# One-token attention decode: the last head's wo in sixteen short transfers on ScalarE's queue during block 30

## The chip, the cores and the metric

One core of a Trainium2 chip runs the kernel. The metric is the device time of one execution in microseconds (us). Five engines take part: TensorE (PE, whose weight loads are shown apart as PEld), VectorE (DVE), ScalarE (ACT), GpSimd (POOL) and SyncE (SP). Bulk data move on the core's 16 DMA engines; SP and ACT issue transfers to them, each on a queue of its own (q1 and q10 in the profile).

## The reference

One token's attention over a cache of 65,536 positions with 16 query heads and 8 KV heads, mixed by a gate with a small token MLP:

```python
q = (x @ wq) ...                       # x: 1 x 448, wq: 448 x 4096
scores = einsum("bhqd,bhkd->bhqk", q, k) * Dh ** -0.5   # Dh = 256, 2 query heads for each KV head
o = einsum("bhqk,bhkd->bhqd", softmax(scores), v)
a = o.reshape(1, 1, 16 * 256) @ wo     # wo: 4096 x 448
b = token_mlp(B_x)                     # layernorm, w1, gelu, w2
g = sigmoid((x * gate_w).sum(-1))
return g * a + (1 - g) * b
```

All inputs are bf16. K and V together are 537 MB; everything else is small beside them.

## The kernel before

The cache is cut into 32 blocks of 16,384 positions (four for each KV head). For each block, SP loads K into two thirds of `k_all` and V into `vt`; DVE transposes K in eight steps (`transposes`, L410), PE forms the scores (`scores`, L418), `softmax` (DVE, PE, and the exp on ACT at L506) updates a running maximum and sum, and PE multiplies by V (`pv`, L438).

Blocks 0 to 29 run in a loop, two for each turn; blocks 30 (`L - 1`) and 31 (`L`) are written out behind it. The order of each engine's instructions is the program's order (`seq` ties each to the one before). SP's transfers of the tail are, in that order: V rows 0 to 48 of block 30 (L135), the two halves of K of block 31 (L127, one into each free third of `k_all`), V rows 48 to 128 of block 30 (L135), seven V pieces of block 31 (`load_v_last`, L161: 64, 32, 16, 8, 4, 2 and 2 rows of each partition), wo of the last head (`load_wo`, L152), and the result (L705).

wo of the other heads comes in a wide form (`load_wo_wide`, L144) and is spread by PE and two casts on ACT (`spread_wo`, L563 and L567). Head 14's is spread directly behind the loop, by `spread_wo(0)`. The last head's is loaded in place, into the second half of `wo_sb`:

```python
            load_v_last(L)
            load_wo(HQ - 1, 1)
```

It is read by the last matmuls (L697): PE finishes the products of the last V pieces (`columns`, L463), DVE scales them into `oT` (L691), PE multiplies `oT` by `wo_sb`, DVE and ACT copy the two halves of the row (L703, L704), and SP writes it out.

A built program gives each transfer of SP and ACT one of eight completion counters in turn, in the order of the program, and makes a transfer wait until the earlier one on its counter has landed.

Of the kernel before, what the change touches and what calls it, by code (L numbers as in the profile page):

```python
# [14 lines left out]
HQ = 16  # L15
# [18 lines left out]
def kernel(  # L34
# [15 lines left out]
    nc = tc.nc  # L50
# [12 lines left out]
    def seq(ins):  # L63
        e = ins.ins.engine
        if e in last:
            tc.add_manual_dep(
                ins.ins,
                last[e],
                mybir.DependencyInfo(
                    mybir.DependencyClass.NoSync, mybir.DependencyReason.DATA  # L70
                ),
                reason="program order",
            )
        last[e] = ins.ins.name
        return ins
# [7 lines left out]
    wo_sb = kvpool.tile([128, REP, 2, D], BF16, name="wo_sb")  # L83
# [42 lines left out]
    def load_k(n, h, slot):  # L126
        seq(nc.sync.dma_start(  # L127
            out=slots[slot], in_=rows("k", n)[:, h * KP:(h + 1) * KP, :]
        ))
# [4 lines left out]
    def load_v(n, j0=0, j1=VP):  # L134
        seq(nc.sync.dma_start(out=vt[:, j0:j1, :], in_=rows("v", n)[:, j0:j1, :]))  # L135
# [15 lines left out]
    def load_wo(h, r):  # L151
        seq(nc.sync.dma_start(  # L152
            out=wo_sb[:, r],
            in_=A_wo.rearrange("(h p c) n -> h p c n", p=128, c=2)[bass.ds(h, 1)].rearrange(
                "o p c n -> (o p) c n"
            ),
        ))

    def load_v_last(n):
        for j0, j1 in LAST:  # L160
            seq(nc.sync.dma_start(  # L161
                out=v_half[j0 // KP][:, j0 % KP:(j1 - 1) % KP + 1, :],
                in_=rows("v", n)[:, j0:j1, :],
            ))
# [3 lines left out]
        out=wq_t[:, :], in_=A_wq[DM:D, :].rearrange("r (h n) -> (r h) n", h=2)  # L168
# [8 lines left out]
    for n0, n1 in ((0, D // 2), (D // 2, D)):  # L177
        seq(nc.scalar.dma_start(
            out=gw[:, n0:n1], in_=gate_w.rearrange("(o n) -> o n", o=1)[:, n0:n1]
# [14 lines left out]
        out=val[:], in_=rowsel[:, :, :, 0:NI], op=ALU.add, axis=AXIS.XY  # L194
    ))
    fst = const.tile([128, 2, REP], FP32)
    for e in range(2):
        seq(nc.vector.tensor_reduce(
            out=fst[:, e, :], in_=rowsel[:, :, :, e:e + 1], op=ALU.add, axis=AXIS.XY
# [3 lines left out]
        out=par[:], in_=ident_f[:].rearrange("p (a r) -> p r a", r=REP), op=ALU.add, axis=AXIS.X  # L203
# [3 lines left out]
        out=nval[:], in0=val[:], scalar1=-scale, scalar2=None, op0=ALU.mult  # L207
# [7 lines left out]
        out=same[:], in_=val[:].unsqueeze(1).to_broadcast([128, 64, REP])  # L215
# [8 lines left out]
        out=sel[:],  # L224
        in_=ident.rearrange("p (w k) -> p w k", w=NW).unsqueeze(2).to_broadcast([128, NW, NQ, 32]),
# [7 lines left out]
        out=xrr[:], in_=xr[:, DM:D].unsqueeze(2).to_broadcast([1, D - DM, 2])  # L233
    ))
    x_col = hd_ps[:, 40:44]
    for k in range(3):
# [13 lines left out]
        out=xtm[:], in0=par[:], scalar1=x_col[:, 3:4], scalar2=None, op0=ALU.mult  # L250
# [19 lines left out]
        out=veps[:], in0=mv[:, 1:2], scalar1=1e-5, scalar2=None, op0=ALU.add  # L270
# [5 lines left out]
    for _ in range(2):  # L276
# [3 lines left out]
            out=ntmp[:], in0=ntmp[:], scalar1=-0.5, scalar2=1.5, op0=ALU.mult, op1=ALU.add  # L280
# [3 lines left out]
        out=h_bc, in0=xf, scalar1=mv[:, 0:1], scalar2=rstd[:, 0:1],  # L284
        op0=ALU.subtract, op1=ALU.mult,
    ))
    for b in range(NF):
        seq(nc.scalar.activation(
            out=gel[b], in_=h_bc, func=ACT.Gelu_apprx_tanh,
# [33 lines left out]
    for k in range(2):  # L323
        seq(nc.vector.tensor_copy(
            out=qq[:, :, :, k, :], in_=qq_ps.rearrange("p (w g r) -> p w g r", g=HKV, r=REP)
# [30 lines left out]
    def mixer_tail():  # L356
        seq(nc.vector.tensor_scalar(
            out=gate[:], in0=ez[:], scalar1=1.0, scalar2=None, op0=ALU.add
        ))
        seq(nc.vector.reciprocal(out=gate[:], in_=gate[:]))  # L360
        seq(nc.vector.tensor_copy(out=b2f[:], in_=b2b[:]))
        seq(nc.vector.tensor_scalar(
            out=y_sb[:], in0=y_ps, scalar1=b2f[0:1, 0:1], scalar2=None, op0=ALU.add
        ))
        seq(nc.vector.tensor_scalar(
            out=rest[:], in0=y_sb[:], scalar1=gate[0:1, 0:1], scalar2=None, op0=ALU.mult
        ))
        seq(nc.vector.tensor_tensor(out=rest[:], in0=y_sb[:], in1=rest[:], op=ALU.subtract))
# [57 lines left out]
    def score_block(e, pair, hooks={}, order=FORWARD):  # L426
        for k, i in enumerate(order):
            transposes(pair, i)
            scores(e, i, k == 0, k == NI - 1)
            if k in hooks:  # L430
                hooks[k]()

    def pv(n, ip, jjs=range(NJ), tile=None, dst=pv_ps, last_ip=NI // 2 - 1):
        pT = pT_tiles[n % 2]
        v = vt[:, 32 * ip:32 * (ip + 1), :] if tile is None else tile
        for jj in jjs:
            grp = jj % 4
            seq(nc.tensor.matmul(  # L438
                dst[32 * grp:32 * grp + 2 * REP, :, :],
                lhsT=pT[:, 32 * jj + 2 * REP * ip:32 * jj + 2 * REP * (ip + 1)],  # L440
                rhs=pairs(v)[:, :, jj, :],
                start=(ip == 0 and jj < 4),
                stop=(ip == last_ip and jj >= NJ - 4),
                tile_position=(0, 32 * grp),
            ))

    def pv_one(n, i):
        ip, e = divmod(i, 2)
        for jj in range(NJ):
            grp = jj % 4  # L450
            seq(nc.tensor.matmul(
                pv_ps[32 * grp:32 * grp + 2 * REP, e, :],
                lhsT=pT_tiles[n % 2][:, 32 * jj + 2 * REP * ip:32 * jj + 2 * REP * (ip + 1)],
                rhs=vt[:, NJ * i + jj, :],
                start=False, stop=False,
                tile_position=(0, 32 * grp),
            ))
# [60 lines left out]
    def accumulate(e, src=pv_ps):  # L518
        seq(nc.vector.scalar_tensor_tensor(  # L519
            out=acc[:], in0=acc[:], scalar=al_tiles[e][:, 0:1], in1=src[:, :, :],  # L520
            op0=ALU.mult, op1=ALU.add,
        ))
# [37 lines left out]
    def spread_wo(r):  # L560
        for c in range(2):
            for u in range(WS):
                seq(nc.tensor.matmul(  # L563
                    wo_ps[c], lhsT=steps[:, WS - u:WS - u + 128], rhs=wo_in[:, 2 * u + c, :],
                    start=(u == 0), stop=(u == WS - 1),
                ))
            seq(nc.scalar.copy(out=wo_sb[:, r, c, :], in_=wo_ps[c]))  # L567
# [13 lines left out]
    def gate_column():  # L581
        seq(nc.tensor.matmul(
            sm_ps[:, 200:201], lhsT=ones_f[0:1, :], rhs=gate[0:1, 0:1], start=True, stop=True
        ))
        seq(nc.vector.tensor_copy(out=gcol[:], in_=sm_ps[:, 200:201]))
# [47 lines left out]
                products(e)  # L633
    last.clear()
    spread_wo(0)
    mixer_tail()
    gate_column()
    result_base()

    for n in (L - 1, L):  # L640
        if n < L:
            score_block(0, (0, 1), order=UPPER_FIRST)
        else:
            score_block(1, (2, 1), {2: lambda: pv(L - 1, 0), 3: lambda: pv_one(L - 1, 2)})
        if n == L - 1:
            load_v(n, 0, 48)
            load_k(L, 0, 2)
            load_k(L, 1, 1)
            load_v(n, 48, VP)
        else:  # L650
            load_v_last(L)
            load_wo(HQ - 1, 1)
        if n < L:
            softmax(n % 2)
        else:
            def rest_base():
                for k in range(2):
                    seq(nc.tensor.matmul(
                        f_rows[k], lhsT=ident_f[0:1, 0:1], rhs=base[0:1, k * MC:(k + 1) * MC],
                        start=True, stop=False, tile_position=(0, 32 * k),  # L660
                    ))
                pv(L - 1, 2, range(4, NJ))

            softmax(n % 2, [lambda: pv_one(L - 1, 3), lambda: pv(L - 1, 2, range(4)), rest_base])
            seq(nc.vector.tensor_scalar(
                out=lsv[:], in0=val[:], scalar1=lsum[:, 0:1], scalar2=None, op0=ALU.mult
            ))
            pv(L - 1, 3)
            accumulate((L - 1) % 2)
            seq(nc.tensor.matmul(  # L670
                sm_ps[:, 456:456 + REP], lhsT=ones_f[:, :], rhs=lsv[:, :], start=True, stop=True
            ))
            seq(nc.vector.reciprocal(out=rdv[:], in_=sm_ps[:, 456:456 + REP]))
            seq(nc.vector.tensor_scalar(
                out=rdv[:], in0=rdv[:], scalar1=gcol[:, 0:1], scalar2=None, op0=ALU.mult
            ))
# [5 lines left out]
    for c in range(2):  # L682
# [9 lines left out]
        out=oT[:], in0=o_last, in1=rdv[:].unsqueeze(1).to_broadcast([128, 2, REP]), op=ALU.mult  # L692
# [43 lines left out]
```

## Time and profile before

| | |
|---|---|
| median of 3 runs | 1263.91 us (1263.62 to 1263.98) |
| span of the profiled execution, first to last instruction | 1261.8 us |
| beside the span, to the median | 2.1 us |
| PE, DVE, ACT busy | 824.5, 711.8, 75.7 us |
| DMA | 544.36 MB, mean 431 GB/s |

The profile's page stands on one execution; only its span is given, so its own time is taken as the span and the 2.1 us that the median has beside it. Shares of the chain are shares of the span in which the work that ended last was waiting for the thing named. "DMA share" in the windows is the mean busy share of the 16 DMA engines; it can go a little over 1 in a short stretch, since a packet counts where it starts. A DMA row with three figures gives the count, the size, and the us from issue to landing.

### The profile page before, as it was taken

The page shows a single profiled execution, that of the slowest core. Times are in us where ns is not written, and L with a number is a line of the kernel's source. Part 1 is how long each engine was busy: PE and PEld are TensorE (multiplying, and loading weights), DVE is VectorE, ACT ScalarE, POOL GpSimd, SP SyncE. Part 2 cuts the span into 40 slices and gives each one's busy share as a digit, 9 for nine tenths or more (in the row PEclk, how much of TensorE's full clock was granted, in tenths as well). Part 3 has the DMA queues.
Part 4 walks back from the last instruction along what each step waited for, and adds up shares of the span by engine and source line. Part 5 has one row for each costly group of instructions (what it writes and reads, how often), then busy time and mean ns, then how long its engine had stood idle before and what let it go on. Part 6 is the DMA issues. An engine that isn't in the chain of part 4 may idle for free.

```text
span 1261.8 us, 12358 instructions
## 1 busy us (share of the span) xinstructions
PE 824.5 (65%) x4818; PEld 331.2 (26%) x4818; DVE 711.8 (56%) x755; ACT 75.7 (6%) x163; POOL 4.8 (0%) x9
## 2 busy tenths in 40 slices
PE   4757467575666756577566766658656576665668
PEld 2222122222222312223222322223222232222224
DVE  5665456654556644566544665445655456654575
ACT  4000000000000000000000000000000000000000
POOL 1000000000000000000000000000000000000000
PEclk8887788877787877978778887788877797877878
DMA  9999999999999999999999999999999999999998
GB/s 415 435 435 432 439 432 432 437 434 437 432 434 435 434 425 440 416 441 443 423 434 437 432 432 439 432 439 432 432 439 432 439 432 432 439 432 435 421 435 355
DMA packets 11624, 544.36 MB, mean 431 GB/s; under 512 B 1532, under 2 KB 1918, under 8 KB 2782
## 3 DMA queue, kind: packets, MB, share of 16 engines
q1 hardware_dynamic: 11522, 544.22, 99.6%
q8 instruction: 6, 0.10, 0.0%
q14 instruction: 4, 0.03, 0.0%
q10 hardware_dynamic: 92, 0.01, 0.0%
HBM read 544.22 MB, written 0.00 MB: 431 GB/s over the span
## 4 chain that ended last, share of the span: by engine, by line
DMA 67%; PE 14%; DVE 13%; issue 4%; ACT 0%; SPq 0%; DVEq 0%; ACTq 0%
DMA k_all<-in_A_k_cache_dram 67%; PE sc L418 13%; DVE kT L410 13%; PE hd_ps L463 0%; PE pv_last L438 0%; PE pv_last L563 0%; PE f L563 0%; DVE rmax L475 0%; PE hd_ps L684 0%; ACT p_sb L506 0%; PE hd_ps L554 0%; PE pv_ps L438 0%; PE f L697 0%; PE sm_ps L493 0%; DVE pT L513 0%
## 5 line engine op out<-in xcount | busy, mean ns | idle before, releaser
L418 PE MATMUL sc<-kT,qz 128*128 128x512 bf16 x2048 | 550.4, 419 | 315.0 <-DVE kT L410 314.8
L410 DVE STREAM_TRANSPOSE kT<-k_all 128x2048 f32<-128x2048 f32 x256 | 571.3, 2283 | 207.6 <-DMA k_all<-in_A_k_cache_dram 154.7
L418 PEld LDWEIGHTS <-qz 128*128 128x128 bf16 x2048 | 212.5, 104 | 651.3 <-issue 474.8
L438 PE MATMUL pv_ps<-vt,pT 128*4 128x512 bf16 x1968 | 172.0, 525 | 27.3 <-DVE pT L513 27.3
L519 DVE SCALAR_TENSOR_TENSOR acc<-acc,al,pv_ps 128x512 f32<-128x512 f32 x31 | 23.2, 747 | 160.4 <-PE pv_ps L438 160.4
L438 PEld LDWEIGHTS <-pT 128*4 128x4 bf16 x2000 | 56.5, 108 | 130.1 <-issue 83.9
L506 ACT ACTIVATE p_sb<-sc,nb 128x512 bf16<-128x512 f32 x32 | 22.0, 687 | 1020.0 <-DVE nb L502 1020.0
L475 DVE TENSOR_REDUCE rmax<-sc 128x1 f32<-128x512 f32 x32 | 22.1, 692 | 63.7 <-PE sc L418 63.7
L513 DVE STREAM_TRANSPOSE pT<-p_sb 128x512 bf16<-128x512 bf16 x32 | 22.8, 712 | 27.1 <-ACT p_sb L506 27.1
L525 PE MATMUL hd_ps<-lsum,same 128*128 128x1 f32 x30 | 8.2, 342 | 28.8 <-DVE lsum L514 28.8
L493 PE MATMUL sm_ps<-mrun,ones_f 1*128 1x2 f32 x64 | 12.1, 256 | 21.2 <-DVE mrun L492 13.0
L479 PE MATMUL sm_ps<-ident_f,rmax 128*1 128x128 f32 x32 | 8.6, 270 | 24.5 <-DVE rmax L475 24.5
L563 PE MATMUL pv_last<-wo_in,steps 128*128 128x448 bf16 x64 | 15.6, 368 | 5.5 <-PEq L605 5.5
L563 PEld LDWEIGHTS <-steps 128*128 128x128 bf16 x128 | 11.6, 101 | 22.6 <-issue 14.4
L493 PEld LDWEIGHTS sm_ps<-mrun,ones_f 1*128 1x128 f32 x64 | 9.4, 182 | 27.4 <-DVE mrun L492 16.3
L567 ACT CAST wo_sb<-pv_last 128x448 bf16<-128x448 f32 x16 | 8.5, 532 | 126.3 <-PE pv_last L563 126.3
L558 DVE TENSOR_TENSOR a_acc<-a_acc,hd_ps 1x448 f32<-1x448 f32 x15 | 9.1, 608 | 12.3 <-PE hd_ps L554 12.3
L554 PE MATMUL hd_ps<-wo_sb,oT 128*1 128x448 bf16 x60 | 15.8, 351 | 0.0
L563 PE MATMUL f<-wo_in,steps 128*128 128x448 bf16 x64 | 15.5, 367 | 0.0
L570 ACT COPY wo_sb<-wo_sb 128x896 bf16<-128x896 bf16 x15 | 14.1, 937 | 14.5 <-PE hd_ps L554 14.5
L525 PEld LDWEIGHTS hd_ps<-lsum,same 128*128 128x128 f32 x30 | 6.9, 285 | 30.1 <-DVE lsum L514 30.1
L550 DVE CAST oT<-hd_ps 128x2 bf16<-128x2 f32 x15 | 2.4, 160 | 20.8 <-PE hd_ps L540 20.8
(124 smaller groups left out, 194.6 us busy)
## 6 DMA issues: line engine op xcount, KB each, us to landing
k_all<-in_A_k_cache_dram SPq DMA_DIRECT2D x2, 4096.0 KB, 15.2
vt<-in_A_v_cache_dram SPq DMA_DIRECT2D x1, 5120.0 KB
k_all<-in_A_v_cache_dram SPq DMA_DIRECT2D x1, 4096.0 KB
wo_in<-in_A_wo_dram SPq DMA_DIRECT2D x15, 224.0 KB, 27.8
vt<-in_A_wq_dram SPq DMA_DIRECT2D x1, 3072.0 KB, 10.4
vt<-in_A_v_cache_dram SPq DMA_DIRECT2D x1, 3072.0 KB
k_all<-in_A_v_cache_dram SPq DMA_DIRECT2D x1, 2048.0 KB
k_all<-in_A_v_cache_dram SPq DMA_DIRECT2D x1, 1024.0 KB, 21.7
```

The source lines that it names most:

```text
L410: seq(nc.vector.transpose(out=kT_tiles[i % 2][:].rearrange("p j w k c -> p (j w k c)").bitcast(FP32), in_=slots[pair[i // 4]][:, i % 4 * N ...
L418: seq(nc.tensor.matmul(sc_tiles[e][:, :], lhsT=qz[:, 2 * w + c, 2 * (NI - i):2 * (NI - i) + 128], rhs=kT_tiles[i % 2][:, :, w, :, c], star ...
L438: seq(nc.tensor.matmul(dst[32 * grp:32 * grp + 2 * REP, :, :], lhsT=pT[:, 32 * jj + 2 * REP * ip:32 * jj + 2 * REP * (ip + 1)], rhs=pairs( ...
L475: seq(nc.vector.tensor_reduce(out=rmax[:], in_=sc_ps[:, :], op=ALU.max, axis=AXIS.X))
L493: seq(nc.tensor.matmul(sm_ps[:, 128:128 + REP], lhsT=ones_f[0:1, :], rhs=mrun[0:1, :], start=True, stop=True))
L506: seq(nc.scalar.activation(out=p_sb[:, :], in_=sc_ps[:, :], func=ACT.Exp, scale=scale, bias=nb[:, 0:1], accum_out=den[:, 0:1],))
L513: seq(nc.vector.transpose(out=pT[:, :], in_=p_sb[:, :]))
L519: seq(nc.vector.scalar_tensor_tensor(out=acc[:], in0=acc[:], scalar=al_tiles[e][:, 0:1], in1=src[:, :, :], op0=ALU.mult, op1=ALU.add,))
L525: seq(nc.tensor.matmul(hd_ps[:, 460:461], lhsT=same[:].rearrange("p a r -> p (a r)"), rhs=lsum[:, 0:1], start=True, stop=True,))
L554: seq(nc.tensor.matmul(a_ps, lhsT=oT[:, c, r:r + 1], rhs=wo_sb[:, r, c, :], start=(r == 0 and c == 0), stop=(r == REP - 1 and c == 1),))
L563: seq(nc.tensor.matmul(wo_ps[c], lhsT=steps[:, WS - u:WS - u + 128], rhs=wo_in[:, 2 * u + c, :], start=(u == 0), stop=(u == WS - 1),))
L570: seq(nc.scalar.copy(out=wo_sb[:, 0], in_=wo_sb[:, 1]))
```

## The change

wo of the last head (128 rows of 1,792 bytes) is no longer one transfer of SP behind the last V piece. ACT issues it behind the casts of `spread_wo(0)`, as sixteen transfers of 8, 15, 14, ... 2 and 1 rows, while block 30 is worked on.

```diff
+    def load_wo_rows(h, r):
+        p0 = 0
+        for k in (8, *range(15, 0, -1)):
+            seq(nc.scalar.dma_start(
+                out=wo_sb[p0:p0 + k, r],
+                in_=A_wo.rearrange("(h p c) n -> h p c n", p=128, c=2)[h, p0:p0 + k],
+            ))
+            p0 += k
...
     spread_wo(0)
+    load_wo_rows(HQ - 1, 1)
     mixer_tail()
...
             load_v_last(L)
-            load_wo(HQ - 1, 1)
```

## The prediction

> **What bounds the kernel now.** I read the page's chain first, then the rate of the DMA engines in the steady loop, then the chain in order of time over the tail, then SP's own timeline.
>
> ```profile
> DMA 67%; PE 14%; DVE 13%; issue 4%; ACT 0%; SPq 0%; DVEq 0%; ACTq 0%
> 1100.00:1190.00 90.00, 59.20 (x343) 23.55 (x345) 48.35 (x60) 4.88 (x12) 0.00 (x0) 0.80 1.00 434
> ...
> 1170.69 28.98 DMA k_all<-in_A_k_cache_dram
> 1199.77 2.32 DVE kT L410
> ...
> 1231.38 2.32 DVE kT L410
> ...
> 1255.67 2.55 PE hd_ps L463 x96
> 1258.25 0.17 DVE oT L691
> 1258.46 0.95 PE f L697 x8
> 1259.42 0.37 DVE res L703
> ```
>
> The first row is the share of each engine in the chain: two thirds are waits for K. The second is a stretch of 90 us: the last two figures say that the 16 DMA engines are busy all the time (1.00) at 434 GB/s, so an engine moves 27.1 GB/s. The time of this kernel is its bytes at that rate, plus what stands behind the last byte. K of block 30 lands at 1170.69 + 28.98 = 1199.67.
>
> ```profile
> 1192.95 0.34 SPq L135 DMA_DIRECT2D vt<-in_A_v_cache_dram  x1
> 1193.40 17.95 SPq L127 DMA_DIRECT2D k_all<-in_A_k_cache_dram  x2
> 1211.44 0.38 SPq L135 DMA_DIRECT2D vt<-in_A_v_cache_dram  x1
> 1219.79 17.87 SPq L161 DMA_DIRECT2D k_all<-in_A_v_cache_dram  x7
> 1238.31 0.33 SPq L152 DMA_DIRECT2D wo_sb<-in_A_wo_dram  x1
> L127 SPq DMA_DIRECT2D k_all<-in_A_k_cache_dram x2: 328/344/360, 1193.4 to 1211.0; - x2
> L161 SPq DMA_DIRECT2D k_all<-in_A_v_cache_dram x7: 327/328/424, 1219.8 to 1237.2; - x7
> ...
> vt<-in_A_v_cache_dram SPq DMA_DIRECT2D x1, 3072.0 KB
> k_all<-in_A_k_cache_dram SPq DMA_DIRECT2D x1, 4096.0 KB, 15.2
> k_all<-in_A_v_cache_dram SPq DMA_DIRECT2D x1, 128.0 KB, 20.7
> wo_sb<-in_A_wo_dram SPq DMA_DIRECT2D x1, 224.0 KB
> ```
>
> SP issues far ahead: the second half of the last K goes out at 1211.0 and lands 15.2 us later, at 1226.2; the last V piece goes out at 1237.2 and lands 20.7 us later, at 1257.9. Half 2 is 4096 KB, 4.19 MB, 9.66 us at 434 GB/s, so half 1 landed at about 1226.2 - 9.66 = 1216.6; forward from K of block 30 it is the same (3.15 MB of V in 7.25 us and half 1 in 9.66 us: 1216.6). The wo transfer comes behind the last V piece and delays nothing but itself. PE's last product of V ends at 1258.22, 0.3 us after that piece: DMA and PE end together. Four of those 96 products take 2.55 / 96 x 4 = 0.11 us, so PE has 0 to 0.2 us in hand; I take 0.1.
>
> **The change, part by part.** *What is removed.* One issue by SP at 1238.3, and 224 KB from behind the last V piece, where nothing waited for them. Gain: at most what the last product (L697) waited for wo. It starts 0.04 us after its operand oT: nothing, at most some 0.1 us between its eight matmuls.
>
> *What is moved.* The same 0.23 MB now come ahead of K's halves and all V pieces. At 434 GB/s that is 0.53 us on the mean engine. A transfer of k rows occupies k engines, so one engine carries from 0 to 16 rows: 0 to 1.05 us. [...]
>
> *What the built program adds.* Every transfer of SP and ACT takes the next of eight completion counters, and waits until the counter's earlier transfer has landed. Sixteen more transfers turn the counters round. The order of the changed program, with the waits that are new:
>
> ```
> ACT  row transfer 1 (15 rows)       counter 5
> SP   first K half  (L127)           waits for row transfer 1        counter 5
> ACT  row transfer 6 (10 rows)       waits for K of block 30
> ACT  row transfer 7 (9 rows)        waits for V 0:48 of block 30
> SP   second K half (L127)           waits for the FIRST K HALF      counter 5
> SP   V 48:128 (L135)                behind it on SP's queue
> ```
>
> Before, the first half waited for a transfer of the kernel's start, and the second for none of the tail: it was bound by DVE and issued at 1211.0, 5.6 us before half 1 had landed.
>
> *First K half, later.* What the wait takes is read from the start of the kernel, where ACT's short transfers also ran beside a full SP queue, of 24 KB rows:
>
> ```profile
> 0.74 0.42 SPq L167 DMA_DIRECT2D vt<-in_A_wq_dram  x1
> 0.74 0.53 ACTq L166 DMA_DIRECT2D xr<-in_A_x_dram  x1
> 1.30 0.34 ACTq L176 DMA_DIRECT2D tables<-in_B_w_dram  x1
> 2.03 0.10 PEld L237 LDWEIGHTS <-xr 1*128 1x128 bf16 x1 [2.03 <-DMA xr<-in_A_x_dram]
> vt<-in_A_wq_dram SPq DMA_DIRECT2D x1, 512.0 KB, 3.2
> ...
> q1 hardware_dynamic: 16, 0.39, 157.4%
> q10 hardware_dynamic: 14, 0.00, 2.6%
> ...
> q1 hardware_dynamic: 16, 0.39, 189.0%
> q10 hardware_dynamic: 14, 0.00, 1.6%
> ```
>
> The last four rows are the packets of 4.2 to 4.8 us and of 5.2 to 5.7 us (q1 is SP's queue, q10 ACT's); between the two stretches no packet starts. One 14-row transfer gives 14 packets beside 16 of SP's, so on 14 engines, one each; then each engine does one SP row (24 KB, 0.9 us), and then comes ACT's packet with the counter. A short transfer thus needs two turns, each behind one SP row. ACT's second cast of wo ends at 1195.17 and the issues follow it:
>
> ```profile
> 1194.64 0.53 ACT L567 CAST wo_sb<-f 128x448 bf16<-128x448 f32 x1 [0.23 <-PE f L563]
> 1223.87 0.69 ACT L506 ACTIVATE p_sb<-sc,nb 128x512 bf16<-128x512 f32 x1 [28.70 <-DVE nb L502]
> ```
>
> Transfers 0 and 1 need four turns: the first behind a 64 KB row of K (65.5 KB / 27.1 GB/s = 2.4 us at most), three behind 24 KB rows (2.8 us). From 1195.2 with 1.3 us to the first byte (below), transfer 1 lands by about 1202, and the first half goes out 8 to 9 us later than now. The queue needs it when V 0:48 ends, 1199.67 + 7.25 = 1206.9. Covered by some 3 us: cost 0. [...]
>
> *Second K half.* This wait is not covered: nothing stands behind half 1, since V 48:128 is behind half 2 on SP. All 16 engines run dry. Price of a restart from dry: xr, 0.9 KB, is issued at 0.74 and used at 2.03, 1.3 us, with hardly any data; the 512 KB at the start landed 3.2 us after issue, of which 0.52 MB / 434 GB/s = 1.2 us is data: 2.0 us. So 1.3 to 2.0; I take the middle, 1.65, since the first has one row and the second sixteen engines that start unevenly. SP's own step between a wait and an issue: 0.1 (its issues at 1192.95 and 1193.40 stand 0.11 apart, one wait instruction between them).
>
> *Rows ahead of half 1.* Of the 0.53 us, row transfers 0 to 7 go before half 1 lands (two turns of 0.9 to 1.2 us each from 1197 to 1216.6); the rest goes into the dry time. I take 0.35, bounds 0 and 1.05.
>
> *Lag of single engines.* Instruction fetches use the same engines:
>
> ```profile
> q1 hardware_dynamic: 29, 0.95, 113.3%
> q8 instruction: 1, 0.02, 2.9%
> ```
>
> That is 1242 to 1244 us: 2.9% of 16 x 2 us = 0.93 us on one engine. As the queues never run dry, an engine once hit stays late, and the last one sets a landing. Now the one hit at 1242.6 need not be the last one; after the restart all start level, and it is. Between 0 and 0.93: I take 0.9.
>
> *ACT.* Row transfer 7 waits until 1207, the last ones for transfers 6 to 8, at the latest until the dry time at 1217. Exp of block 30 is needed at 1223.87: covered by 6 us; each us beyond would delay block 31's scores.
>
> Sum: 0.35 + 0.1 + 1.65 + 0.9 - 0.1 = +2.9 us on the last V piece and the end. DVE's and PE's work of both blocks has cover until then: half 2 would land at 1228.4, and DVE reads it after the third of block 31's eight transposes (1231.38). The span of 1261.8 becomes 1264.7. The median of the runs is 1263.91, 2.1 us more than the span, which I leave unchanged: 1263.91 + 2.9 = 1266.8.
>
> **Rivals.**
> *B, a second dry spell.* Row transfer 1 lands only when V 0:48 is through (1206.9): half 1 is issued then, and lands 0.1 + 1.65 + 9.66 later, 1218.3 instead of 1216.6 + 0.35: +1.35 more, 1268.2. It decides from a landing of transfer 1 after 1205. For: four turns, each of unknown length behind 64 KB rows. Against: the q10 rows above.
> *C, the restart forgives.* The dry time costs the engines that were ahead more than the last one, and all start level; if no fetch strikes late, the last V piece moves by 0.35 + 0.1 + 1.3 - 0.2 = 1.55: 1265.5, not slower by the bound. It decides where the lag after the restart is under 0.5 us. Against it: the q8 row.
> *D, faster.* The stall does not come and only the wo product gains 0.1 to 0.3: 1263.7. Against: the wait is in the program.
> *E, the change doesn't spread.* The rows of a transfer with an odd count all go to one engine: 128 rows of 1.8 KB at 27.1 GB/s, 8.5 us on one engine: 1272. Against: the 14 packets.
>
> **How the numbers follow.** A measurement of this kernel tells 0.2%, 2.5 us. Forecast 0.65, its own range 1266.0 to 1267.5, of which 0.09 lies under 1266.4; B 0.14; C 0.19; D 0.01; E 0.01. Slower: 0.56 + 0.14 + 0.01 = 0.71; same: 0.09 + 0.19 = 0.28; faster 0.01 (D with more than I see). The range 1265.4 to 1268.4 takes in A, B's and C's likeliest times, and leaves out the ends.
>
> **What would show it.** SP's timeline: the second L127 at 1216.6 to 1217.5 instead of 1211.0, the SP wait put down to the DMA of k_all, and L135 right behind. The windows: DMA share near 0 for over 1 us around 1217.5, full before and after. If L127's second issue stands at 1211, or the share has no hole, the forecast is wrong at its core; a hole at 1205 to 1207 is B; a hole without a later end is C.

## The result, and the profile after

The changed kernel takes 1269.71 us (median of 3 runs, 1269.62 to 1270.14) against 1263.91 before: 5.8 us slower, ratio 1.0046 with an interval of 1.0032 to 1.006. The forecast of 1266.8 had the direction and half the size; the measured time lies outside its range. The profiled execution has a span of 1268.3 us against 1261.8, so the accounts below add up to 6.5, not to 5.8 (the profile after is that of the longest of its three executions, 1270.14). Landings with two decimals, and figures for "the mean engine", are read from the trace's own records: each half of K has sixteen landing records there, the transfer of 15 rows fifteen, taken as one of each engine that carries it, and a transfer has landed with the last of them.

The shares of the chain, from the page of the changed kernel, and the rows that the forecast asked for: SP's and ACT's timeline (start, us, what), and SP's waits (us in total, times, longest).

```profile
DMA 69%; PE 13%; DVE 12%; issue 4%; SPq 0%; ACT 0%; DVEq 0%
```

```profile
1193.84 0.34 SPq L135 DMA_DIRECT2D vt<-in_A_v_cache_dram  x1
1203.91 15.41 SPq L127 DMA_DIRECT2D k_all<-in_A_k_cache_dram  x2
1219.41 0.38 SPq L135 DMA_DIRECT2D vt<-in_A_v_cache_dram  x1
1219.89 18.04 SPq L170 DMA_DIRECT2D k_all<-in_A_v_cache_dram  x7
...
1195.54 21.95 ACTq L162 DMA_DIRECT2D wo_sb<-in_A_wo_dram  x16
```

```profile
SPq L127 <- DMA k_all<-in_A_k_cache_dram: 14.6, 1, 14.6
SPq L127 <- DMA wo_sb<-in_A_wo_dram: 9.6, 1, 9.6
```

Both waits are there. The first half of K goes out 10.5 us later than before (1203.91, not 1193.40), behind a row transfer of wo; the second at 1219.0 instead of 1211.0, behind the first half itself. What the queues did meanwhile stands in the windows (the last two figures are DMA share and GB/s):

```profile
1205.00:1206.00 1.00, 1.00 (x5) 0.31 (x4) 0.05 (x1) 0.00 (x0) 0.00 (x0) 0.61 1.35 482
1206.00:1207.00 1.00, 1.00 (x6) 0.45 (x5) 1.00 (x1) 0.00 (x0) 0.00 (x0) 1.00 0.59 225
1207.00:1208.00 1.00, 0.65 (x4) 0.19 (x2) 1.00 (x1) 0.00 (x0) 0.00 (x0) 1.00 1.16 470
...
1216.00:1217.00 1.00, 0.80 (x4) 0.27 (x3) 1.00 (x2) 0.00 (x0) 0.00 (x0) 1.00 0.55 222
1217.00:1218.00 1.00, 0.91 (x5) 0.42 (x5) 1.00 (x2) 0.00 (x0) 0.00 (x0) 1.00 0.07 23
1218.00:1219.00 1.00, 0.98 (x5) 0.34 (x4) 1.00 (x1) 0.00 (x0) 0.00 (x0) 1.00 0.01 2
1219.00:1220.00 1.00, 0.72 (x4) 0.35 (x4) 0.23 (x1) 0.00 (x0) 0.00 (x0) 1.00 0.34 98
...
1263.00:1264.00 1.00, 0.98 (x36) 0.90 (x33) 0.00 (x0) 0.00 (x0) 0.00 (x0) 0.50 0.07 27
```

There is the hole of the forecast, 1217 to 1219, a dip at 1206, and a last microsecond in which 0.07 of the engines, about one of sixteen, still moves data. The dip is not a hole: a packet counts whole in the microsecond in which it starts, the neighbours have 1.35 and 1.16, and the three together 1.03. Followed from its start to its end, packet by packet, the trace has at least 16 packets under way at every moment from 1203 to 1210. The landings, from the answers on DMA (count, KB, us from issue to landing; the row transfer, the first half, the second half, the last V pieces):

```profile
wo_sb<-in_A_wo_dram ACTq DMA_DIRECT2D x1, 26.2 KB, 8.0
k_all<-in_A_k_cache_dram SPq DMA_DIRECT2D x1, 4096.0 KB, 14.9
k_all<-in_A_k_cache_dram SPq DMA_DIRECT2D x1, 4096.0 KB, 12.0
k_all<-in_A_v_cache_dram SPq DMA_DIRECT2D x2, 128.0 KB, 26.9
```

Transfer 1 landed at 1203.8, half 1 at 1218.85 (2.3 us later than before), half 2 at 1231.00 (4.8 later), the last V piece at 1264.35 (6.45 later). PE follows at once, as before:

```profile
1237.45 26.90 DMA k_all<-in_A_v_cache_dram
...
1264.39 0.28 PE hd_ps L472 x4
...
1264.70 0.17 DVE oT L700
...
1264.92 0.95 PE f L706 x8
...
1265.87 0.37 DVE res L712
```

So three losses: 2.3 us up to half 1, 2.5 us between the halves (12.15 us apart, not 9.66), and 1.7 us from half 2 to the last V piece (33.35 us, not 31.68). By the windows alone one would put the first to the late first half, with its dip at 1206. The packets, and the experiments, say otherwise.

One more row matters: SP's packets of V between 1200 and 1204 us, before and after (packets, MB, share of the 16 engines' time).

```profile
q1 hardware_dynamic: 70, 1.72, 99.8%
```

```profile
q1 hardware_dynamic: 63, 1.55, 97.1%
q10 hardware_dynamic: 54, 0.05, 3.8%
```

Share times 64 us (16 engines for 4 us) over the packets: a 24 KB packet took 0.912 us before and 0.986 us after. The packets of wo (q10) take only 3.8% of the time, yet SP's packets themselves have become longer. Summed over V rows 0 to 48 and half 1, SP's packets take 18.4 us on each engine instead of 17.1; the 1.3 us more, and up to 0.7 us that the rows take themselves (128 packets of 0.079 us and 128 small ones of 0.009, over 16 engines), make up nearly all of what half 1 is late on the mean engine (2.2 us).

### The profile page after: what moved, and what is told of

Same layout as the page of the kernel before. It is cut to its first block, busy times and chain, and to the rows that moved or that the text cites. A ratio compares the mean times of both kernels' runs of the same rounds, so it can differ in the third digit from the quotient of the medians.

```text
span 1268.3 us, 12375 instructions
## 1 busy us (share of the span) xinstructions
PE 825.8 (65%) x4818; PEld 331.9 (26%) x4818; DVE 711.5 (56%) x755; ACT 75.6 (6%) x163; POOL 4.8 (0%) x9
## 4 chain that ended last, share of the span: by engine, by line
DMA 69%; PE 13%; DVE 12%; issue 4%; SPq 0%; ACT 0%; DVEq 0%
DMA k_all<-in_A_k_cache_dram 66%; DVE kT L419 12%; PE sc L427 12%; DMA k_all<-in_A_v_cache_dram 2%; PE pv_last L572 0%; PE hd_ps L563 0%; PE f L572 0%; SPq L170 0%; PE f L706 0%; PE sm_ps L549 0%; ACT p_sb L515 0%; DVE rmax L484 0%; SPq L132 0%; PE hd_ps L549 0%; PE sm_ps L502 0%
```

## The experiments

Each was timed in turns with the kernel before, each of three groups on a chip of its own (medians of the kernel before: 1263.86, 1264.17 and 1263.94). "Theory W" is that the two waits cost the time; "rival R" that the rows themselves do.

### The rows in one transfer

```diff
-        for k in (8, *range(15, 0, -1)):
+        for k in (128,):
```

> wo of the last head at the changed kernel's place on ACT's queue, as one transfer of 128 rows; with one transfer only, neither half of K shares a counter with a transfer that is still under way. Theory W (two waits on shared counters drain the DMA queues, about 2.3 us at 1206, 2.5 us at 1218, and 1.7 us of fetch lag that comes after a restart): first half issued near 1193.4, second near 1211.0, no hole in the DMA share, time within 0.5 us of the kernel before (1263.9 to 1264.4). Rival R (the rows themselves, 0.23 MB in short packets ahead of K and V, slow the stream): 2 us or more slower, 1266 or above.

1264.44 us against 1263.86, ratio 1.0005 (0.9996 to 1.0014). The halves go out at 1194.02 and 1210.22. The packets from 1200 to 1204 us:

```profile
q1 hardware_dynamic: 66, 1.62, 94.1%
q10 hardware_dynamic: 65, 0.12, 7.5%
```

64 x 0.941 / 66 = 0.912 us: the same 128 rows, on the same queue at the same time, with SP's packets unharmed. Half 1 landed at 1217.28, 0.7 us later than before, close to the rows' own time (0.23 MB at 434 GB/s are 0.53 us). R in its plain form falls.

### The first wait, with rows

```diff
-        for k in (8, *range(15, 0, -1)):
+        for k in (8, *range(15, 5, -1), 15):
```

> Twelve row transfers (8, 15, 14, ... 6, and 15 rows) instead of sixteen. The first half of K still waits for row transfer 1; the second half then shares its counter with row transfer 5, which has landed by 1211. Theory W: first L127 at about 1203.9 and a dip of the DMA share near 1206.5, second L127 back at 1211, no hole at 1218; 2.0 to 2.7 us slower than before from the first wait, up to 4.0 if the fetch lag follows it as well: 1266 to 1268. Rival R: as slow as the changed kernel, 1269.5, since the same bytes go the same way.

1267.17 us, ratio 1.0024 (1.0015 to 1.0033).

```profile
1201.83 9.39 SPq L127 DMA_DIRECT2D k_all<-in_A_k_cache_dram  x2
1211.67 0.33 SPq L135 DMA_DIRECT2D vt<-in_A_v_cache_dram  x1
```

```profile
q1 hardware_dynamic: 62, 1.52, 96.5%
```

The second half is back at 1210.9 and the hole is gone. The first half went out 2.1 us earlier than in the changed kernel, yet half 1 landed at 1218.96, no earlier than there (1218.85). So the late issue is not what sets it. The packets are long again: 64 x 0.965 / 62 = 0.996 us. That the time lies in W's 1266 to 1268 is luck: half 1 is late by its packets and not by its wait, and some 0.7 us stand behind the last V piece (4.6 us from there to the end of the span, 3.9 before).

### The second wait with rows, and its control

Seven transfers (16, 16, 16, 16, 16, 16, 32 rows) and six (16, 16, 16, 16, 32, 32), ordered between the two halves:

```diff
             load_k(L, 0, 2)
+            load_wo_rows(HQ - 1, 1)
             load_k(L, 1, 1)
...
+        last[mybir.EngineType.Activation] = last[mybir.EngineType.SP]
-        for k in (8, *range(15, 0, -1)):
+        for k in (16, 16, 16, 16, 16, 16, 32):
```

> wo in seven transfers (six of 16 rows, one of 32) whose counters come between the two halves of K: the first half waits for nothing new, the second shares its counter with the first half. Theory W: first L127 at 1193.4, second behind half 1's landing (1216.9 plus 0.1), DMA share near 0 for over 1 us, then 2.5 us later, 0.3 us of rows, and 0.9 to 1.7 us of fetch lag: 3.5 to 4.5 us slower than before, 1267.4 to 1268.4. Rival R: the hole costs little, and the time is that of the same rows without it (the run with six transfers).

> The control of the run with seven: six transfers (four of 16 rows, two of 32) between the halves of K. The second half of K then shares its counter with V 0:48 of block 30, landed at 1207, before the half's own time at 1211. Same bytes, same queue, same place, one transfer less. Theory W: no hole, 0 to 0.5 us slower than before (1263.9 to 1264.4). Rival R: 2 us or more slower, as with seven.

Seven: 1270.57 us, ratio 1.005 (1.0036 to 1.0064). Six: 1266.32 us, 1.0022 (1.0013 to 1.0031). One transfer more costs 4.25 us: that is the second wait (from half 1 to the last V piece the two profiled executions take 45.6 and 41.4 us). Seven came out above W's 1267.4 to 1268.4, by what the rows cost in both. With six, two of eleven executions stand apart, at 1269.4 and 1269.5; the others lie between 1265.8 and 1266.7. The wait's place, with seven (SP's timeline, then the windows):

```profile
1194.17 25.41 SPq L127 DMA_DIRECT2D k_all<-in_A_k_cache_dram  x2
1219.67 0.38 SPq L135 DMA_DIRECT2D vt<-in_A_v_cache_dram  x1
```

```profile
1218.00:1219.00 1.00, 1.00 (x5) 0.35 (x4) 1.00 (x1) 0.00 (x0) 0.00 (x0) 1.00 0.00 0
1219.00:1220.00 1.00, 0.71 (x4) 0.34 (x4) 0.24 (x1) 0.00 (x0) 0.00 (x0) 1.00 0.00 0
```

The miss is the control: 2.5 us slower with no harmful wait at all, where W allowed 0.5. The packets of the run with six, 1200 to 1204 us:

```profile
q1 hardware_dynamic: 57, 1.40, 93.4%
q10 hardware_dynamic: 57, 0.06, 4.4%
```

1.049 us a packet, and half 1 at 1218.53. With seven, where the first half waits for nothing, half 1 landed at 1219.11. Rows in several transfers delay half 1 by 2.0 to 2.6 us, wait or no wait. R was half right: not the rows, but the way they are cut.

### The second wait without rows

```diff
+    spare = const.tile([1, 7], BF16)
...
             load_k(L, 0, 2)
+            (seven ACT transfers of 2 bytes into spare)
             load_k(L, 1, 1)
```

> The second wait without the rows: wo stays behind the last V piece as in the kernel before, and ACT issues seven spare transfers of 2 bytes into a tile that nothing reads, placed in the order between the halves of K. The second half then shares its counter with the first half, the first half with nothing under way. Theory W (the waits cost the time): hole at 1217 to 1219, half 2 landing 2.5 us later, the fetch lag 1.7 us on top: 3.5 to 4.5 us slower than before, 1267.4 to 1268.4. Rival R (the rows are the whole of it): no more than 1 us slower, below 1265.

1268.62 us against 1264.17, ratio 1.0035 (1.0022 to 1.0048): 4.45 us for one wait.

```profile
1193.30 23.85 SPq L127 DMA_DIRECT2D k_all<-in_A_k_cache_dram  x2
1217.25 0.38 SPq L135 DMA_DIRECT2D vt<-in_A_v_cache_dram  x1
```

Half 1 landed at 1216.68, half 2 at 1228.85, the last V piece at 1262.00: 12.17 and 33.15 us apart. This is three quarters of the loss, and it splits as in the changed kernel: 2.5 us at the hole, 1.5 us after it.

### What makes SP's packets longer

One spare transfer on ACT, at the changed kernel's place, in four shapes; wo stays behind the last V piece:

```diff
+        src = A_wo.rearrange("(h c q) n -> h q c n", c=WC, q=32)[h]
+        seq(nc.scalar.dma_start(out=wo_in[0:16], in_=src[0:16]))
...
+        (the others: wo_in[0:32:4] and wo_in[0:8] with src[0:8], wo_in[0:128:8] with src[0:16])
```

> What makes rows in several transfers slow the stream where one transfer of 128 rows did not? One spare transfer of 128 pieces of 896 bytes on ACT's queue at the changed kernel's place, into partitions 0 to 15 (eight pieces each) of a tile that nothing reads any more; wo stays behind the last V piece. No half of K waits. Theory P (ports: the engine that carries a piece is not the one whose stream fills those partitions): V's 24 KB packets take 0.97 us or more while the pieces run (0.912 before), half 1 lands at 1217.5 or later, 0.7 us or more slower than before. Rival N (the number of transfers and of their completion writes): one transfer, so packets stay at 0.912, half 1 lands by 1217.2, no more than 0.5 us slower.

> One spare transfer of 64 pieces of 896 bytes into partitions 0, 4, 8, ... 28 (eight each), wo as before. [...] Theory P: V's 24 KB packets stay at 0.912 us, within 0.3 us of before. Rival N: the same as with partitions 0 to 7.

> [...] Rival N: no difference between the two.

> [...] If it is foreign partitions as such, as slow as the run with 0 to 15 (packets 1.05 us or more, 1266 to 1272); if it is the crowding on few, packets below 0.95 us and 0.3 to 1 us slower than before.

Theory P assumes that each engine fills partitions of its own (the others are its "foreign" ones), and takes ports for the place. No trace here names the engine of a packet or shows a port. That pieces in steps of four go where their engine writes anyway, from which P's forecasts start, was the author's assumption; the runs show the partitions alone. "Crowded" below means pieces in partitions in a row, "uncrowded" in steps of four. The packets of 1200 to 1204 us, in the order of the expectations:

```profile
q1 hardware_dynamic: 56, 1.38, 97.3%
q10 hardware_dynamic: 56, 0.05, 4.1%
```

```profile
q1 hardware_dynamic: 67, 1.65, 95.5%
```

```profile
q1 hardware_dynamic: 69, 1.70, 99.6%
```

```profile
q1 hardware_dynamic: 68, 1.67, 97.8%
```

| into partitions | V packet, us | half 1 landed | ratio |
|---|---|---|---|
| 0 to 15, 128 pieces | 1.112 | 1220.49 | 1.0044 (1.0027 to 1.0062) |
| 0, 8, ... 120, 128 pieces | 0.920 | 1217.44 | 1.001 (1.0001 to 1.0019) |
| 0, 4, ... 28, 64 pieces | 0.912 | 1217.05 | 1.0005 (0.9996 to 1.0014) |
| 0 to 7, 64 pieces | 0.924 | 1217.93 | 1.0007 (0.9998 to 1.0016) |

One transfer is enough: N falls. Of P the runs show that the partitions matter, and no more. Pieces in steps of four cost the packets nothing (0.912); partitions in steps of eight, or 0 to 7, cost about 1% (0.920 and 0.924); partitions 0 to 15 cost 22% (1.112). Why 0 to 7, with eight pieces in each partition as in the run with 0 to 15, cost so little stays open. Between the two 8-partition shapes the times do not differ by more than their intervals; only the packets do. Partitions in steps of four and of eight came out a little slower than expected, 0.5 us for 0.3 and 1.2 for 1.0; the last was timed on another chip than the other three.

The run with 0 to 15 held a surprise: long after its pieces had landed (by 1208), SP's packets stayed long. From 1222 to 1227 us, with nothing but SP's queue at work:

```profile
q1 hardware_dynamic: 62, 2.03, 108.3%
```

1.083 x 80 / 62 = 1.397 us instead of 1.213; the 40 KB packets that follow are as much longer, until 1241. Two of its executions took 1266.1 and 1266.4 us, the other four, the profiled one among them, 1271.2 to 1272.5; the ratio in the table lies between the two. Why it lasts, and what ends it, stays open.

### The first wait alone, and both waits, without crowding

Spare transfers of 8 rows of 1,792 bytes, twelve with the counters of the run on the first wait and sixteen with those of the changed kernel; and twelve in eight partitions in a row:

```diff
+        for t in range(12):
+            s = t // 8
+            p0 = t % 4 + 32 * (t // 4 % 2)
+            rows8 = slice(p0, p0 + 29, 4)
+            seq(nc.scalar.dma_start(out=wo_in[rows8, 2 * s:2 * s + 2], in_=src[rows8]))
...
+        (in a row: rows8 = slice(8 * (t % 8), 8 * (t % 8) + 8))
```

> [...] The first half of K waits for transfer 1, the second for transfer 5, long landed by 1211. Theory P (rows in partitions that their engine does not itself fill slow the stream; the first wait costs nothing): packets stay at 0.912 and 1.213 us, half 1 lands by 1217.1, 0.2 to 0.7 us slower than before. Rival N (twelve transfers with their completion writes do it): packets 5 to 15% longer, half 1 at 1218 or later, 2 us or more slower. Rival F (the first wait costs 1 us or more by itself): packets at 0.912, yet a dip of the DMA share near 1206 and half 1 later than 1217.5.

> As the run before it with sixteen transfers: the counters are those of the changed kernel, and both halves of K wait as there. Theory W with P: half 1 by 1217.1, a hole, half 2 12.1 us later, fetch lag behind it: 4.2 to 5.0 us slower than before (1268.2 to 1269.0), that is 1 to 1.5 us less than the changed kernel, which has the foreign rows as well. Rival N: as slow as the changed kernel or slower.

> As the run with twelve, but each transfer into eight partitions in a row (0 to 7, 8 to 15, ... 56 to 63): the same counters, bytes and engines, only the partitions differ. Theory P: packets longer than 0.912 us, half 1 0.3 to 1.5 us later than with partitions in steps of four, and the time likewise. Rivals N and F: no difference.

Twelve in steps of four: 1265.39 us, ratio 1.0012 (1.0003 to 1.0021). Sixteen: 1268.82, 1.0038 (1.0024 to 1.0052). Twelve in a row: 1266.33, 1.0021 (1.0011 to 1.003). The packets of 1200 to 1204 us with twelve in steps of four, then in a row:

```profile
q1 hardware_dynamic: 75, 1.84, 106.9%
```

```profile
q1 hardware_dynamic: 73, 1.79, 104.6%
```

0.912 us in the first: twelve transfers leave the packets as they are, with the small ones that go with them (16 of q10's 35 packets in these 4 us are under 512 bytes), and N is gone for good. In a row it is 0.917, and later up to 1.28 where 1.213 is normal; the times (0.9 us apart) have intervals that overlap, and half 1 landed at 1217.64, not later than with steps of four (1217.76), where P asked for 0.3 to 1.5 us. So P is borne out here by the packets alone, and weakly.

The first wait can now be read without crowding. SP's timeline and the windows, twelve first:

```profile
1193.83 0.34 SPq L135 DMA_DIRECT2D vt<-in_A_v_cache_dram  x1
1203.97 7.02 SPq L127 DMA_DIRECT2D k_all<-in_A_k_cache_dram  x2
...
1205.00:1206.00 1.00, 1.00 (x5) 0.40 (x4) 0.00 (x1) 0.00 (x0) 0.00 (x0) 0.69 1.19 452
1206.00:1207.00 1.00, 1.00 (x6) 0.41 (x5) 0.87 (x1) 0.00 (x0) 0.00 (x0) 1.00 0.44 186
1207.00:1208.00 1.00, 0.84 (x4) 0.29 (x3) 1.00 (x1) 0.00 (x0) 0.00 (x0) 1.00 1.24 531
```

```profile
1193.11 0.34 SPq L135 DMA_DIRECT2D vt<-in_A_v_cache_dram  x1
1203.09 14.36 SPq L127 DMA_DIRECT2D k_all<-in_A_k_cache_dram  x2
...
1206.00:1207.00 1.00, 1.00 (x4) 0.38 (x3) 1.00 (x1) 0.00 (x0) 0.00 (x0) 0.50 1.24 533
```

Issued at 1203.97 there is a dip, and half 1 lands at 1217.76; issued at 1203.09 there is none, and it lands at 1216.98. That is what F asked for, and yet it is not F. The dip is again one of counting (1.19, 0.44 and 1.24 in a row; at least 16 packets under way throughout). And of the 0.8 us, 0.7 are there before the half: with twelve, SP issues V rows 0 to 48 already 0.7 us later, ahead of all rows, and their last packet ends at 1207.24 instead of 1206.56. From there, by the mean of the last sixteen packets of each transfer, half 1 takes 9.99 us with twelve, 9.97 with sixteen, and 9.96 with twelve in a row, where it was issued at 1201.28 (9.69 before, without rows). So the first wait cost nothing in any of them, and F falls. The 1.45 us of the run with twelve, more than P's 0.2 to 0.7, are in part behind the last V piece: from there to the end of the span it has 4.65 us, as the other two runs with twelve transfers (4.62 and 4.65), against 3.94 before; why is open.

## Why the prediction was wrong

Its core was right: sixteen transfers turn the counters, the second half waits for the first, the queues run dry, DMA and nothing else sets the end. Every sign asked for is there, the second issue at 1218.99 instead of 1216.6 to 1217.5. The sizes of three terms were wrong, and they add up to the miss: 2.3 us for 0.35, 2.5 for 1.75, and 1.7 for 0.9.

*"Rows ahead of half 1 ... I take 0.35, bounds 0 and 1.05."* This is the step that failed worst. Half 1 came 2.3 us later. In one transfer the rows cost 0.7; cut into transfers of up to 15 or 16 rows they cost 2.0 to 2.6 whether or not the first half waits (the runs with six, seven and twelve). The term counted the bytes of wo and not what they do to the bytes of K and V: a packet of 24 KB went from 0.912 to 0.986 us. The forecast looked at how many engines a short transfer uses, and not at the partitions that it writes. That crowding is what lengthens the packets in the changed kernel is read from the single spare transfers, where partitions alone differ, and from the run with sixteen uncrowded ones; the changed kernel's own transfers of up to 15 rows were not run uncrowded.

*"First K half, later ... Covered by some 3 us: cost 0."* The cost was right, the cover was not. It was reckoned to when V 0:48 ends, 1206.9; but the first engine is done with V at 1205.58, and into empty queues a half's first packet comes some 0.96 us after its issue (below). So the half had to go out by about 1204.6, an estimate, and went out at 1203.91, since transfer 1 landed at 1203.8 and not "by about 1202": 0.7 us of cover, not 3. That it was enough is luck in part. Rival B, with its hole at 1205 to 1207, did not occur: the dip in the windows is one of counting, and with crowded rows half 1 lands at 1218.9 to 1219.1 with the half issued at 1203.9, 1201.8 or 1194.2. By the same estimate B's threshold, a landing of transfer 1 after 1205, was some 0.5 us too late.

*"Price of a restart ... 1.3 to 2.0; I take the middle, 1.65."* Half 2 is 12.0 us from issue to landing, 2.35 more than its 9.66 of data, and SP's step took 0.14 instead of 0.1: 2.5 us, the same in the three other runs with a hole (12.08, 12.17 and 12.12 us between the landings). The forecast took the middle of two rows of the kernel's start, and the larger of them, 2.0, was nearer. In the four kernels half 2's first packet starts 0.95 to 0.97 us after its issue, and the first packet of an engine takes up to 2.06 us where 1.213 is normal.

*"Lag of single engines ... I take 0.9."* Half 2 to the last V piece takes 33.15 to 33.58 us in the four kernels with a hole, and 31.67 to 31.81 in the kernel before, with wo in one transfer, and in the runs with six transfers and on the first wait: 1.5 to 1.9 more with the hole. (The run with twelve in a row has 32.48 without a hole, so some lag comes without it too.) Over the sixteen engines the mean time from half 2 to the end is 31.9 to 32.0 in the four, 31.8 before: hardly any loss. The mean loses at the hole instead, 13.0 to 13.2 us from half to half, not 9.67. So the hole costs some 3.4 us on the mean engine; at its end the engines stand level (in the changed kernel half 2's landing records lie within 0.45 us, half 1's within 2.1), which hides 0.9 of it from the landing of half 2; then some fall behind again, and the last landing shows it. When they fall behind points to the instruction fetches. Two of them, of 16 and 8 KB, start between 1242.0 and 1243.0 in each of the four. In the runs with the transfers of 2 bytes and with sixteen uncrowded ones, V 48:128 lands before them, on all engines within 0.5 us (1240.5 to 1241.0 and 1240.8 to 1241.2); at the landing after them two engines stand 0.7 to 1.6 us behind the others. In the changed kernel V 48:128 is landing as they start, fourteen engines by 1243.2 and two at 1244.1 and 1244.8. Which engine a packet ran on the trace does not say, and no run leaves the fetches out, so the cause is argued and not shown. The rows of 1242 to 1244 us in the changed kernel:

```profile
q1 hardware_dynamic: 45, 0.95, 113.2%
q8 instruction: 1, 0.02, 3.7%
q14 instruction: 1, 0.01, 1.0%
```

3.7% of 16 x 2 us is 1.2 us on one engine, where the prediction had 0.93.

*PE's 0.1 us* was not there: the last V piece moved by 6.45 and the span by 6.5 us. *The cover of everything else* held.

The whole, by the last V piece of the profiled executions: 4.1 us later than before with the second wait alone (1262.00), 4.8 with sixteen transfers that have the changed kernel's counters and waits but uncrowded rows (1262.68), 6.45 in the changed kernel. So the second wait is 4.1, the rows 0.7, crowding some 1.7. The medians (4.45, 4.88 and 5.80) tell the same once it is seen that the first two have 0.5 us more behind the last V piece (4.4 to 4.5 us to the end of the span, 3.9 to 4.0 before and after). Most of it stands between DVE's last result and SP's issue of the output, 0.48 us in these two and 0.08 before and after; why is open.

Rival C fell with the lag. D and E, faster and 1272, did not come; against E, the transfer of 15 rows has fifteen landing records.

## What to carry to other kernels

Short transfers in a full DMA queue were paid for twice here: by the completion counters they take, which made a large transfer wait for its own predecessor (seven transfers instead of six cost 4.25 us), and by the partitions they write (24 KB packets of 1.112 us with 128 pieces in partitions 0 to 15, of 0.912 with twelve transfers in steps of four). So try small data in one transfer over all 128 partitions first: the same move cost 0.6 us that way, no more than the interval leaves open, and 5.8 us in sixteen pieces. Before a dip in a window is called a hole, look at its neighbours. And price a dry queue on the mean engine, not on one landing: here it levelled the engines, and 1.5 to 1.9 us of the loss appeared only at the landing of the last V piece.

## What the runs showed of the hardware

SP's packets were slowed by another queue's writes far beyond the time that these take: 128 pieces of 896 bytes, 4% of the engines' time, made 24 KB packets 22% longer (1.112 us for 0.912) when they went into partitions 0 to 15, and 15% longer packets (1.397 us for 1.213) lasted some 33 us beyond the last piece. Into partitions in steps of eight the same 128 pieces left the 24 KB packets at 0.920 us, so the partitions decided. Where on the way to them the time is lost was not measured.

The price of a dry queue was not the gap in the windows: in the changed kernel the share is near 0 for 2 us (0.07 and 0.01), half 2 lands 2.5 us later, and the mean engine lost 3.5.
